# Transposing layer-normed rows by DMA instead of TensorE, and keeping split weights in DRAM, in a four-layer attention kernel

## The chip, the cores and the metric

The kernel runs on one core of a Trainium2 chip. The metric is the device time of one execution in microseconds (us), as the median of several runs. Profiles come from one further execution, recorded by the hardware profiler.

The core has five engines with instruction queues of their own: PE (TensorE, the matrix engine; its weight loads are a row of their own, PEld), DVE (VectorE), ACT (ScalarE), POOL (GpSimd) and SP (which here only issues DMAs). An engine takes its instructions strictly in order. Semaphores make it wait for the others.

## The reference

Four layers of multi-query attention over x of 2048 rows by 512 columns, 32 heads of 16 dimensions, one key head and one value head shared by all. Layers 0 and 2 use the weights A, layers 1 and 3 the weights B.

```python
def layer(x, wq, wk, wv, wo):                    # x: 1, 2048, 512
    q = (x @ wq).reshape(B, S, 32, 16).transpose(0, 2, 1, 3)
    k, v = x @ wk, x @ wv                        # one head of 16 each
    p = softmax(einsum("bhqd,bkd->bhqk", q, k) * 16 ** -0.5)
    o = einsum("bhqk,bkd->bhqd", p, v)
    return o.transpose(0, 2, 1, 3).reshape(B, S, 512) @ wo

x = x + layer(layernorm(x), A); x = x + layer(layernorm(x), B)
x = x + layer(layernorm(x), A); x = x + layer(layernorm(x), B)
```

All is float32. The softmax needs 4 x 32 x 2048 x 2048 exponentials.

## The kernel before

**Number formats.** A float32 operand of a projection is split into two float16 parts, high and low (`hi = float16(w)`, `lo = float16(w - hi)`). A product of two such operands is three float16 matmuls per chunk of 128 (`three`, L538). Probabilities and values stay float32.

**Units of attention.** The rows are four blocks of 512 queries, the heads four groups of eight, which makes 16 "pairs" per layer and 64 in all. Scores are computed in *halves*: a tile of 128 by 1024 float32, 64 halves to a pair, 4096 in all. A half goes one of two ways. With `score` (L858) PE writes one of two buffers `st` of PSUM and ACT takes the exponential into one of 16 tiles `pt` (L868). With `score_v` (L875) PE writes the bank `by_v` in two parts, and DVE works out the exponential: L902 twice, then a chain of five instructions (L916, L918, L919, L920, L913). `pv` (L928) multiplies the tiles `pt` with the values into two accumulators `acc`. Its matmuls, like those of the scores, use one 64-row half of the PE array each, and `both` (L519) issues work for the two halves together, so that they run beside each other.

**Everything else** goes through one more PSUM bank, `beside`: the projections for keys and values (kv), for the queries (one product per block and head group), the output projections, and, before the change, the transposes of x. A product is 12 float16 steps on each half of the array, taken step by step between the scores, or 12 whole-array steps (`whole`, L562). DVE must empty the bank before the next item may use it.

**Layer norm** of one block (`add_normed`, L592): for each of four tiles of 128 rows, DVE takes the statistics, POOL the power for the standard deviation, and DVE writes the normed rows `xn` (`norm`, L415). PE transposes each tile by four 128 by 128 float32 transposes into `beside` (`transposes`, L423). DVE then reads the bank twice: it writes the high part of `xnT` (L432) and subtracts to get the low part (L434). The first block of layer 0 has a path of its own ahead of the rest; 15 blocks, or 60 tiles, go through `add_normed`.

**Weights.** `add_load` (L580) loads a matrix (`wq` for the queries, `wo` for the output) in four chunks of float32, and DVE splits each chunk (`w_hi` L372, `w_lo` L377); the columns of `wq` are also reordered, and its low part takes four instructions. Since layers 2 and 3 use the same matrices as layers 0 and 1, and SBUF holds one set, each is loaded and split again there. `wq` of layer 0 is made ahead of the main part.

**The order** of the work is written out by hand in one string, `ORDER` (L58): each letter is a step, and the Python code that builds the kernel walks along it once. "S" is a score by ACT. Lower-case letters are pairs of actions for the two array halves: "E" and "O" stand for pv, "M" and "N" for one or two product steps, "V" and "W" for score_v (so "a" is pv on both halves, "l" and "m" on one, "p" and "q" a product step on one, "r" and "s" score_v on one). "P" is a whole-array product step, "F" another whole item on PE (a transposed tile, the transposes for v, query lengths), "X" the next item of DVE's list, "I" DVE's L902, "0" and "1" the next step of a DVE chain, "Q" the load of the next pair's queries, "G" and "D" the emptying of accumulators and the division, "Y" a read of `beside` by DVE that lets a bank change array halves. `plan` (L710) makes the two lists, for PE and DVE, from which P, M, N and F, and X, take the next item; an item names how far the other list must be. The string fixes each engine's own order; between engines only the data dependences count.

**DMAs.** Nearly all are issued by SP, in the order of the string. `spaced` (L807) spreads a row of them: the later ones are issued some exponentials later, each made to wait for an exponential shortly before. Queries go through DRAM (`q_rest` L479 stores them, `load_q` L821 loads them replicated). x lies in DRAM between uses (`load_x` L394, `out_add` L499).

Of the kernel before, what the change touches and what calls it, by code (L numbers as in the profile page):

```python
# [63 lines left out]
    "pSbm0SppspmSIppmpSYGeoSGrqqqlSIql0qqSc0lqS0maSa0lSpmppmXSlmSQXaXaSXFXSmaXXlXXSX0eqSlqqlqSrqqqlSYmIdpGpSp"
    "sdpSpmppSpImdpSYlGqqlS0qqaXSaXlSm0ap0SdnSQd0ppmSpmp0ppSmapSYlmqSlqqqlSrqolSqqlqSIqeXaSaXSadpSGppmSYGieIq"
    "Sem0Se0qlqS0qlmSQc0lqSma0SlmlqSlYmpSmpppmSkbISpmlXSfXaSIalSGpmpd0SpmnGSpppS0pm0bSa0lSmaSQ0lqqeSqlqqSclqS"
    "qaSclmSXaXSfaSlmlIsSImlSGFSXXa0aS0lmqSXqlXmlSGqlqqS0aaSQXa0SpmppmXpSb0pSpmdXpSXpdYlSqgqqSXXlmXeSqlmSqalX"
    "GSmqSXaaXSaIqSlGqqqrScIeSYm0ap0SQb0pSpmpmp0SbnmS0dlSmalSsYqlqSqIclXSmaSXalSpmppmSpGYmlSqqGrcISc0lqSoe0Sl"
    "0maSQl0mSppmpmDDp0SpmppSdaSYqelSmfXlXSaIpSdppsSpmIdpSpmYl0Sqqc0lSGmqSGc0lqSqqlqSDlmDaDSQlmS0almSDDb0pSda"
    "SYqalSXmgXSaIaSlmrSFSIXlmfGSppmInSGppspS0pmIaS0dl0SsalSQ1mdp0SalS1ma1Sqee0SqcS0aeSqqlIqS0lmmrSeIlqSGmmrS"  # L70
    "0aIaSGglS0daISXaS1mgXlSm1ap1SpmnSm0ndSppmDpS0bmlSmDlDSlm0lmSloIqSc0eSqqrlDDqS0qlmScIlmXSmrXlSmlIpm0Snm0s"
    "pSpmIppSpm0aSls1dS0alSb1mS1alSm0aScIeSDqqeS0qalSDqqlDjSmIaS0alSmk0lS0maS0lmlSIqqlmXSlmXlSm0ppmSpbDD0Spmr"
    "pmSIppmpSY0lsmlIqSql0mS0clqSml0jSqqlqISQa0aSa0Smr0aS0qalSqlDmS0qlmlSmDlDmSaIlSGdpmSXagGSlSXlmIa0SFSXrmlS"
    "XpmppmSppmpSpm0dpSIpmpp0Slm0lmSlmXX0SccXSql0qqSceXSqlsqSDDlmIaXSlm0Smg0lS0maSaIlS0marSIlmS0lmmlS0mgS0alS"
    "Ima0SrmlISlm0lmSrml1Sma0Sa0lSmIaS0gmlSIaS0mglS1ma0SlmS0alm0SmSIa0aSrmSIa0lmSrmlS0maISaXgSmS0mIal0SslmS1l"
    "mSQ0aa1SS0aaISSGrlGSIma0lSslm0SalSm1aS0lmSIalm0SrmXSIlmml0SrS1a0aSS1a0aSlmISlm0SmalXSsSXmaIlSXmlsSaXSaaS"
    "SXXaa0SqqqS1qel0qSqoS0cIeSm0aSrmlISpmn0mrSdn1Sd0bSb0pSmlXa0SpmnSbId0SppsdSIppm0pSmlgS0mlISql0qqlq0SqrqeS"
    "IloqS0qilSXmaS1ppm0ppSmpppmISpm0ppS0malS0mrlSqqloISqe1eSQ0oreSql0mS0almSlImS0pmpgSmIaS0gmlSImeSGllSXXrmG"
    "mSIaXlSsDlmSX0lmmlDDSmlS1maXlS1mlSX0aXaS0lmSaXXlmSlm1SlmmXl0SmlS1almSX0lmSaIaSDDlmXSXF0SfaISaXlSXsaSXF0S"
    "XalmISlmXrSXXFISXmlsS0aXaS0FSlSXXaS0PPPS1PP0SPPP0SP0PSPPSImaXlSXmlSXmlXFXSlmXrSXXmXlXImpS0ppmrSma1lS0mlS"  # L80
    "qlq0loISeq0qSqal0SqqeSa0aSQlmDSpmlDmpDSsppmIpSpmp0pSkmlISma0l0SmrlSqIlmSXagXSml1mpS1ppmpSGlpSGb1dSal0Spm"
    "dS1alSm0aSqlIqlqS0qcrSqqlIqSl0mfS0al0qSqlmSIlml0qSslmSIal0mSpspmSXlmlXSml0pmS0pmnS0pmppmS0pmlSpmdIlS0mlr"
    "SmlImSDDc0jS0ce0SqqlqSIeml0SqlmS0qglmSlmISYmg0nSXmaSXlml0Spm0bSppmIpSpm0aSpmlDSpmDlmDrSmpIlSm0lsSa0lmS0q"
# [1366 lines left out]
```

## Time and profile before

| | before |
|---|---|
| median of 3 runs | 3433.49 us (3431.62 to 3435.33) |
| the profiled execution's own time | 3427.37 us |
| its span, first to last instruction | 3425.6 us |
| granted TensorE clock | 1.000 |
| busy: PE, DVE, ACT | 3357.2, 3251.7, 3382.0 us |
| exponentials on ACT, halves on DVE | 3658, 438 |
| DMA | 147.81 MB, mean 43 GB/s |
| first exponential starts | 24.70 us |

A row of a group of instructions reads: line, engine, operation, output <- input, shape, count | busy time in us, mean length of one in ns | idle time of the engine just before them, and what ended it. Lengths of instructions overlap on an engine (an exponential lasts 1102 ns, the next one starts earlier), so a busy time is not count times length. In a table by stage, each engine has its busy time and, in brackets, the number of its instructions. A row of waits reads: who waited <- for whom, us in total, times, longest. A row of the timeline: start, length, engine, line, what, count, and in square brackets the idle time before it.

### The profile page before, as it was taken

The page shows a single profiled execution, that of the slowest core. Times are in us where ns is not written, and L with a number is a line of the kernel's source. Part 1 is how long each engine was busy: PE and PEld are TensorE (multiplying, and loading weights), DVE is VectorE, ACT ScalarE, POOL GpSimd, SP SyncE. Part 2 cuts the span into 40 slices and gives each one's busy share as a digit, 9 for nine tenths or more (in the row PEclk, how much of TensorE's full clock was granted, in tenths as well). Part 3 has the DMA queues.
Part 4 walks back from the last instruction along what each step waited for, and adds up shares of the span by engine and source line. Part 5 has one row for each costly group of instructions (what it writes and reads, how often), then busy time and mean ns, then how long its engine had stood idle before and what let it go on. Part 6 is the DMA issues. An engine that isn't in the chain of part 4 may idle for free.

```text
span 3425.6 us, 206570 instructions
## 1 busy us (share of the span) xinstructions
PE 3357.2 (98%) x97707; PEld 2087.9 (61%) x97707; DVE 3251.7 (95%) x4436; ACT 3382.0 (99%) x3688; POOL 133.3 (4%) x137
## 2 busy tenths in 40 slices
PE   9999999999999999999999999999999999999998
PEld 5666566555566766646556666664646666554554
DVE  7889999999999999999998999999999899999998
ACT  8999999999999999999999999999999999999997
POOL 3000000000000000000000000000000000000000
PEclk9999999999999999999999999999999999999999
DMA  3221011011012111101001211110101211111010
GB/s 111 63 80 48 32 42 46 28 33 41 30 46 61 49 49 39 42 23 45 23 30 58 59 48 38 42 43 23 47 19 36 67 47 37 35 48 31 23 43 21
DMA packets 119315, 147.81 MB, mean 43 GB/s; under 512 B 32888, under 2 KB 81016, under 8 KB 118456
## 3 DMA queue, kind: packets, MB, share of 16 engines
q1 hardware_dynamic: 116888, 133.65, 13.3%
q8 instruction: 765, 12.53, 1.5%
q10 hardware_dynamic: 1568, 0.85, 0.1%
q14 instruction: 94, 0.77, 0.1%
HBM read 90.57 MB, written 34.59 MB: 37 GB/s over the span
## 4 chain that ended last, share of the span: by engine, by line
PE 60%; ACT 26%; DVE 10%; issue 2%; DMA 1%; SPq 0%; DVEq 0%; ACTq 0%
PE acc L532 31%; ACT pt L868 26%; PE st L532 16%; PE beside L532 9%; PE by_v L532 2%; DVE pt L902 1%; DVE poly L919 1%; DVE poly L920 1%; DVE pt L913 1%; DVE mant L916 1%; PE beside L426 1%; DVE pt L918 1%; PE beside L569 0%; DMA rec<-rs 0%; SPq L1051 0%
## 5 line engine op out<-in xcount | busy, mean ns | idle before, releaser
L868 ACT ACTIVATE pt<-st 128x1024 f32<-128x1024 f32 x3658 | 3367.8, 1102 | 18.4 <-PE st L532 14.4
L532 PE MATMUL acc<-pt,vop 64*32 64x256 f32 (+1 forms) x51728 | 2888.1, 434 | 3.0 <-DVE sum L1017 2.0
L532 PE MATMUL st<-qt,kop 64*32 64x512 f16 x29264 | 1756.6, 380 | 46.1 <-ACT pt L868 25.2
L532 PEld LDWEIGHTS acc<-pt,vop 64*32 64x32 f32 x51728 | 1328.0, 106 | 248.6 <-DVE sum L1017 11.5
L532 PEld LDWEIGHTS <-kop 64*32 64x32 f16 x32768 | 794.3, 90 | 921.5 <-issue 643.7
L902 DVE TENSOR_SCALAR pt<-by_v 128x512 int32<-128x512 f32 x876 | 597.0, 681 | 33.1 <-PE by_v L532 28.2
L913 DVE SCALAR_TENSOR_TENSOR pt<-poly,pt 128x1024 f32<-128x1024 f32 x438 | 535.4, 1222 | 3.4
L920 DVE SCALAR_TENSOR_TENSOR poly<-poly,mant 128x1024 f32<-128x1024 f32 x438 | 534.7, 1222 | 3.1
L919 DVE SCALAR_TENSOR_TENSOR poly<-mant 128x1024 f32<-128x1024 f32 x438 | 533.5, 1219 | 0.0
L532 PE MATMUL beside<-xnT,wq 64*32 64x512 f16 x5760 | 437.4, 376 | 1.6 <-DVE qs L481 0.4
L532 PE MATMUL beside<-wo,ot 64*32 64x512 f16 x5472 | 406.1, 376 | 0.6 <-DVE gqk L497 0.3
L532 PE MATMUL by_v<-qt,kop 64*32 64x512 f16 x3504 | 350.6, 376 | 3.3 <-DVE pt L902 1.8
L918 DVE TENSOR_SCALAR pt<-pt 128x1024 int32<-128x1024 int32 x438 | 303.9, 694 | 4.6
L916 DVE TENSOR_SCALAR mant<-pt 128x1024 int32<-128x1024 int32 x438 | 301.0, 688 | 6.3
L532 PEld LDWEIGHTS <-wq 64*32 64x32 f16 x5760 | 169.8, 92 | 49.1 <-issue 11.7
L532 PEld LDWEIGHTS <-ot 64*32 64x32 f16 x5472 | 159.5, 92 | 40.0 <-issue 5.0
L477 POOL TENSOR_TENSOR sq<-qs 128x512 bf16<-128x512 f16 x64 | 73.6, 1150 | 872.1 <-DVE qs L474 872.1
L532 PE MATMUL beside<-xnT,wkv 64*32 64x512 f16 x1344 | 97.7, 376 | 0.0
L1017 DVE COPY sum<-acc 128x512 f32<-128x512 f32 x126 | 84.0, 686 | 12.0 <-PE acc L532 8.7
L413 POOL TENSOR_TENSOR rstd<-var,nhalf 128x4 f32<-128x4 f32 x15 | 21.7, 1445 | 1451.5 <-DVE var L412 1451.5
L474 DVE TENSOR_SCALAR qs<-beside 128x512 f16<-128x512 f32 x62 | 42.6, 688 | 18.1 <-PE beside L532 9.1
L998 DVE COPY seen<-beside 128x1 f32<-128x1 f32 x92 | 14.3, 155 | 40.4 <-PE beside L532 35.2
(124 smaller groups left out, 831.0 us busy)
## 6 DMA issues: line engine op xcount, KB each, us to landing
qt<-qs SPq DMA_DIRECT2D x236, 128.0 KB
qs<-qs SPq DMA_DIRECT2D x127, 128.0 KB
rec<-rs SPq DMA_DIRECT2D x63, 256.0 KB
qt<-qs SPq DMA_DIRECT2D x26, 512.0 KB
xs<-xt SPq DMA_DIRECT2D x48, 256.0 KB
xt<-xs SPq DMA_DIRECT2D x48, 256.0 KB
sum<-sum SPq DMA_DIRECT2D x252, 32.0 KB
xt<-in_A_x_dram SPq DMA_DIRECT2D x30, 256.0 KB
```

The source lines that it names most:

```text
L426: PE.transpose(ps[:, c * P:(c + 1) * P], xn[:, c * P:(c + 1) * P], ident)
L474: V.tensor_scalar(qs[:, 0], ps, BIG, -BIG, ALU.min, ALU.max)
L477: G.tensor_tensor(sq, qs[:, 0], qs[:, 0], ALU.mult)
L532: PE.matmul(o[32 * j:32 * j + 32], w[j][h], x[j][h], start=start, stop=stop, skip_group_check=True, tile_position=(64 * r, 32 * j))
L868: e = A.activation(pts[:, i], st[s], AF.Exp, scale=SCALE / UP / UP).ins
L902: w = V.tensor_scalar(e[:, 512 * r:512 * r + 512], by_v, SCALE / UP / UP * LOG2E * 2.0 ** 23, LEAD, ALU.mult, ALU.add).ins
L913: writer[i] = V.scalar_tensor_tensor(p, poly, C0, p, ALU.add, ALU.mult).ins
L916: lambda: V.tensor_scalar(mant.bitcast(I32), e, 0x3FFFFF, 0x3F800000, ALU.bitwise_and, ALU.bitwise_or),
L918: lambda: V.tensor_scalar(e, e, 0x7FC00000, HALVES, ALU.bitwise_and, ALU.bitwise_or),
L919: lambda: V.scalar_tensor_tensor(poly, mant, C2, mant, ALU.add, ALU.mult),
L920: lambda: V.scalar_tensor_tensor(poly, poly, C1, mant, ALU.add, ALU.mult),
L1017: V.tensor_copy(sums[pr, odd], acc[odd])
```

## The change

It has four parts.

**Transposes.** The normed rows `xn` are split in SBUF: DVE casts them to float16 (`row_hi`), and later subtracts (`row_lo`). Each of the two parts, 128 rows by 512 columns, is transposed by a DMA of SP into its place in `xnT` (`turned`). PE's transposes and their use of `beside` go. `norm` and the list of `add_normed` are regrouped in pairs of tiles.

**Weights.** Split parts are stored in DRAM the first time (`keep_w`, one store per chunk and part; for `wq` of layer 0 all eight, spaced by three exponentials, at the start of the main part). For layers 2 and 3 `reload_w` loads the eight pieces, spaced by two exponentials, and DVE does nothing.

**Room.** A pool `rws` is added, and the room reserved for dynamic DMAs (`dynamic_dma_scratch_size`) is set to 4096. No DMA of the kernel is issued by POOL.

**The order.** `ORDER` is new throughout. Counted by letter, old to new: S 3658 to 3657, X 772 to 740, F 93 to 33, P 72 to 108, Y 92 to 101, I 876 to 878, G, D and Q unchanged. The two strings begin and end as follows.

```
old: QXPPPPPPPSSPPPPPSXmXlSPPSPPSPPSPPsSPPSIPPSXflmXSaIlSm0aS0FXSmaXlSXmlXSQmaXXlS
new: QXSSPPPPPPSPPPSmrISPPPSmXlsSXlmIeSqqlqSq0e0lq0SqqclS0mSlm0mlSpmbSpmppSYmllqSQ
...
old: SmlIlSDsaISlm0mrSlSD0mal0Sa0SlmSIlm0mSlsS0lmaISa0Slm0Sa0aSS0maS0lmalDaa
new: Sa0SrmlmSIlm0gSa1Sa0lmSlm0Sa0aSa0SS0mSlmIlSmarSalSmaSlImalS000a0a0aa
```

```diff
+    rws = ctx.enter_context(tc.tile_pool(name="rws", bufs=4))
...
+    wscr = {(n, i): [scr.tile([P, NC, D], F16, name=f"{n}{i}{k}") for k in range(2)]
+            for n in ("wq", "wo") for i in range(2)}
+
+    def keep_w(key, c):
+
+        def save(c, k):
+            return lambda: SP.dma_start(wscr[key[0], key[1] % 2][k][:, c], wt[key][k][:, c])
+
+        spaced([save(x, k) for x in c for k in range(2)], 3 if len(c) > 1 else 0)
+
+    def reload_w(key):
+        begin_w(key)
+        spaced([lambda c=c, k=k: SP.dma_start(wt[key][k][:, c], wscr[key[0], key[1] % 2][k][:, c])
+                for c in range(NC) for k in range(2)], 2)
...
+    def turned(l, b, t, k, rows):
+        SP.dma_start_transpose(xnT[l, b][k][:, :, t * P:(t + 1) * P], rows)
+
+    def row_hi(l, b, t):
+        hi = rows_of[l, b, t] = rws.tile([P, D], F16, name="xhi")
+        V.tensor_copy(hi, xn_of[l, b, t])
+        turned(l, b, t, 0, hi)
+
+    def row_lo(l, b, t):
+        lo = rws.tile([P, D], F16, name="xlo")
+        V.tensor_tensor(lo, xn_of.pop((l, b, t)), rows_of.pop((l, b, t)), ALU.subtract)
+        turned(l, b, t, 1, lo)
...
     def add_load(key, chunks=range(NC)):
+        if key[1] >= 2:
+            return work.add_dve("wd", lambda: reload_w(key), 0)
         for c in chunks:
             if c == 0:
                 work.add_dve("wl", lambda: (load_w(key, 0), load_w(key, 1)), 0)
             work.add_dve("wh", lambda c=c: w_hi(key, c), 0)
-            work.add_dve("w", lambda c=c: (w_lo(key, c), c + 2 < NC and load_w(key, c + 2)), 0)
+            work.add_dve("w", lambda c=c: (w_lo(key, c), keep_w(key, [c]), c + 2 < NC and load_w(key, c + 2)), 0)
...
-        n0 = work.add_dve("xr", lambda: norm(l, b, 0), 0)
-        n1 = work.add_dve("xn", lambda: norm(l, b, 1), 0)
-        for t in range(4):
-            add_whole("t", lambda t=t: transposes(l, b, t, beside), n0 if t == 0 else n1)
-            work.add_dve("hi", lambda t=t: xnT_part(l, b, t, 0, beside))
-            n = work.add_dve("lo", lambda t=t: xnT_part(l, b, t, 1, beside), key=("end",))
-            n0 = n1
-            if t < 2:
-                n1 = work.add_dve("xn", lambda t=t: norm(l, b, t + 2), 0)
-            if t == 1:
+        for t0 in (0, 2):
+            for t in (t0, t0 + 1):
+                work.add_dve("xm" if t else "xq", lambda t=t: norm(l, b, t), 0)
+            if t0:
                 add_next_x(l, b)
+            for t in (t0, t0 + 1):
+                work.add_dve("xh", lambda t=t: row_hi(l, b, t), 0)
+            for t in (t0, t0 + 1):
+                n = work.add_dve("xo", lambda t=t: row_lo(l, b, t), 0)
         return n
...
     with tc.manual_schedule():
+        keep_w(("wq", 0), range(NC))
...
-    nc = _bacc.Bacc("TRN2", target_bir_lowering=False, num_devices=1)
+    nc = _bacc.Bacc("TRN2", target_bir_lowering=False, num_devices=1,
+                      dynamic_dma_scratch_size=4096)
```

More of the change, by code (lines that the diff above doesn't have):

```diff
@@ L64 @@
[L64 to L83, printed above, removed]
@@ new lines @@
+    "XaXSXFSXaXXXaXXSsSGlXGSXaIaSXlXmrSXmlImSXlmlXS0maX0Sa0lSmSXaXaXSQXSXaXaXSa0SaSGlGSXXml0SsalSXmXmXSaXlSIm"
+    "SrmIaSlS0a0a0SSa0aSQpmn0SmpppSpmdYlSqqeSqclSGqrGoSIceSsYpmnSmplmSIXaXSXmaXlSXFSXaXXXaX0Spm0ppSd0bSQpmp0p"
+    "Sbmp0SaaSlYGqqSqlqlqqSjeqSceSmImSGXaXlSsaqSqIeqlSq00loS0qelqSm0aSal0SQmndSdnSddpSpmppYSclSXmslXSaIlqSGqq"
+    "jSIqeaSq0eGeSo0eS0aaS0aSb0pmpSdnSQpmdpSppXmaSaXSalqqSqelqSqrqlqSqqlmSYGpdnISpmdSYGclsYSpIpmpSpmppmS0XalS"
+    "0maXlS0FSQXXlmS0bbS0bpSpmdpSpmYlSoiXlXSqcXSXcIeSqqlqSYlmXlmXSpmSGrlGSXmaXlXSmaSalSQmaXXlXSmlSIbdSY0eql0q"
@@ new lines @@
+    "Soe0SrqqeISoqS0lmml0SmSpkbSpImdpS0lGpSGdmXSa0lSXmlm0SQce0SqlqqScDD0lqSqaSYpbmpSppmpSpsmlSpmdpSYcIlSYmdlX"
+    "SmlXSaGcSqjGqSmDeISlqDmlDSQqlq0qSa0a0SaSpm0apSpmn0SmppspSDDmaIlSYqYrmlSqIlmSY0a0lsSdIaGSlpSGb0fSalSImlXm"
+    "SQl1fSXaDaS1FDSDmalXSml0Solqlq1SqloS0aeSmlImS0lmSpmGppkSGnpSId0aSlm0pSs0alSId0dSalS0rmlmSIqlqe0SqflS0maI"
+    "Slm0lS0mlmpSlXsmSIlmlXSrm1qlq0SqeqSql1ml1SmlqSqe0lqSma0SlmlISpm0lmSpsppmISpmp0pSspmp0pSd0dlSml0SalmISe0m"
+    "SlmrSIqalSXmfXlSm0eSIqel0qSql0mSqlm0lSqqlmS0ceSsaDDSYqlImlSrY0m0bS0pbSmnIdS0pmlkSpmIdSXlml1SQrmXlmS0ceSD"
@@ new lines @@
+    "qqeS0qeDlmDSqcIlSm0aSlmDDl0SpspmpSIpmd0pSslpmSGnm0pSllGSIma0pS0lmrSpmlImS0lmrSma0lSqlmXSlmIlSXma0SFDSDml"
+    "DmlSXmlSXmlqqlSqqlqSqe0lqS0oeSlm0aSlmXXS0pmpnsSImpppmXSps0pmpS0dlS0mapSaIlS0marSDDlqImS0agSaISXlmaSr0mlS"
+    "Imlm0Sf0lSa1aS0lmSa1aS0aSaIaS0mgSlmIlS0maSsa1l0SmlSlm0aISlm0Salm0SrmlSmIaSQ0agS0mSIa0aSGrSGllISm0aSflXS1"
+    "mal0SmlS1maS0alSImS0salISmS0rma1SlS0malISm0lsS0lmSaIa0SrSa1a0SSImalXSmlsSXlmSIa0aXSsSa0aSS0mal1Sml0SlmSI"
+    "a0aS0rSaIa0SrSaXaXSlmSlmXSlmmSlSXXa0bSpppSIpm0b0SppsmpISpml0SsalS1ml0Slqqql1qSql0oSce0ScSXlma0SqcSIqeDlq"
@@ new lines @@
+    "SQ0qqrqlSqcISlYm0h0Spmpp0SbdSIppmp0SpmdSXlmSGpmpGppsSppp0mSppmIpSpmdSY0cl0qSoj0lSqqlIqSc0eSmaXXSaDlDSmlX"
+    "mS0alsSmXlISXlmf0SlmX0lSmXaS0lmlSXmIlmS0alSXma0SlmlsXSXmIlS0lmmrS0lmlXSmIaS0alSmXaXSlXmXlSsXlmSIlmXml0Sf"
+    "lSm1aSXXa1lSXmmXS0alSImSXaXlsSImlmS0rmlSm1aS0lS1maS0lSIbb0SknSIdd0pSrmppSDDm1llS0mlS0eoe0SQqcSIce0SscSIl"
+    "mXaSXslmSGFXSXaXaSlSGXlmXXXaX0SppmpSDbpmDSnDmpSIbd0Sf0lSlImlm0SrqqlqS0qeqSqe0lqSqqlqS0lmXlmSXlmSDDb0dpIS"
+    "b0pSspbISpm0aSfl1Sml0lmSqlq0qSc0eSqcISc0lsSqlmISlDmf1SlmDlDSpmlm1SlXmSDDaXlm0SqlqqScIlq0SoeS0qelqSma0Sls"
@@ L230 @@
+    "aSaIaSGSGgl0SmImS0glmS1mS0malS1S0aaISa0SarSDDaIa0SsSa1a0SSIaa0Slm0SrmlSIa0aSsS1a0aSS0aIaDSlmDSDrmlSIa0aS"
+    "rS0aaS1lmS0lmSImal0SsS0malIS0sSa1aS0lmSlmISm0al0SrSImal1SsS0aa0SaSlm0SIa0aSrSIa0aSsS1a0aSSIa0aS0rmlSmlIS"
+    "1lmmS0rlSma0lSS0lmIaGSsSGllISm1aSr1mlS0almS1mSa0aSa0SlmSIlmmS0slSIlmml0SsaSIaSDD0rmaISlS00salSm1S0malS0m"
+    "lSaS0a0aSaISlm0rSlmImlS0rSmaIl0Smg0SlmISmg0lSmSD0SS0SD0aaDSaIa0Sa0SrmlmSIlm0gSa1Sa0lmSlm0Sa0aSa0SS0mSlmI"
+    "lSmarSalSmaSlImalS000a0a0aa"
 )
@@ L350, in fast_path @@
     stat = {}
-    xn_of = {}
+    xn_of, rows_of = {}, {}
     sq_of = {}
```

295 lines of the change are left out of this document (144 added, 151 removed).

## The prediction, made before the changed kernel was run

> **What bounds the kernel now.** I read the page's totals first, then the groups of instructions, then the busy time by stage, then the waits, and last the timeline of both ends.
>
> ```profile
> span 3425.6 us, 206570 instructions
> PE 3357.2 (98%) x97707; PEld 2087.9 (61%) x97707; DVE 3251.7 (95%) x4436; ACT 3382.0 (99%) x3688; POOL 133.3 (4%) x137
> ...
> PE 60%; ACT 26%; DVE 10%; issue 2%; DMA 1%; SPq 0%; DVEq 0%; ACTq 0%
> ...
> L868 ACT ACTIVATE pt<-st 128x1024 f32<-128x1024 f32 x3658 | 3367.8, 1102 | 18.4 <-PE st L532 14.4
> ```
>
> ACT is busy 99% of the span, nearly all of it in 3658 exponentials (L868). Yet the chain of waits goes through PE for 60% and through ACT for 26%: two full engines hand work to each other through two score buffers. How well this goes is seen by stage, in the column of ACT (busy, then count):
>
> ```profile
> core 0: us, PE busy (x) PEld busy (x) DVE busy (x) ACT busy (x) POOL busy (x), PEclk, DMA share, GB/s
> 25.00:1025.00 1000.00, 984.83 (x28888) 616.96 (x28894) 937.69 (x1309) 995.54 (x1082) 42.10 (x39) 1.00 0.16 48
> 1025.00:1225.00 200.00, 199.24 (x6295) 137.31 (x6293) 190.20 (x257) 198.43 (x215) 10.46 (x10) 1.00 0.20 55
> 1225.00:1925.00 700.00, 688.69 (x20002) 421.92 (x19984) 667.56 (x917) 696.91 (x758) 23.29 (x17) 1.00 0.14 40
> 1925.00:2325.00 400.00, 398.23 (x12471) 266.40 (x12458) 389.02 (x534) 398.23 (x433) 18.11 (x15) 1.00 0.16 44
> 2325.00:3025.00 700.00, 685.99 (x19761) 416.05 (x19751) 671.79 (x896) 697.85 (x760) 20.76 (x16) 1.00 0.14 39
> 3025.00:3405.00 380.00, 367.16 (x10113) 210.28 (x10101) 369.10 (x460) 379.54 (x415) 0.00 (x0) 1.00 0.10 31
> ```
>
> One exponential on each border is counted twice, so the paces are 1000/1081 = 0.925 us, 0.935, 0.925, 0.926, 0.922 and, in the last layer, 380/414 = 0.918. PE is busy 99.6% in the slowest stage and 96.6% in the quickest. If every stage ran at 0.918 instead of the mean 3380/3658 = 0.924, the kernel would win 3658 x 0.006 = 22 us. This is about all that relief of PE and DVE can give while ACT keeps its exponentials. Counted in the two order strings, these go from 3658 to 3657: DVE takes 439 halves instead of 438, though the change frees it.
>
> **The change part by part.** Profiled, the kernel took 3427.4 us (the span and 1.8 us around it); the median of the three timed runs is 6.1 us more. The sum is made on the first and carried over with that difference.
>
> *One exponential fewer on ACT*: -0.9 us, at the mean pace.
>
> *The start.* The old string issues seven whole-array products ahead of the first scores:
>
> ```profile
> 22.61 1.69 PE L569 MATMUL beside<-xnT,wq 128*128 128x512 f16 x7 [0.71 <-DVE gv L469]
> 24.22 0.63 PE L532 MATMUL st<-qt,kop 64*32 64x512 f16 x16
> 24.70 26.24 ACT L868 ACTIVATE pt<-st 128x1024 f32<-128x1024 f32 x28 [4.92 <-PE st L532]
> 24.78 1.25 PE L569 MATMUL beside<-xnT,wq 128*128 128x512 f16 x5
> 18.91 0.57 SPq L830 DMA_DIRECT2D qt<-qs  x1
> GB/s 0 0 0 0 0 0 183 156 342 19 0 0 0 0 55 284 371 393 284 11 44 205 208 186 58 0 0 0 0 197 229 415 339 300 339 322 246 240 164 186
> ```
>
> The new one begins with two scores. These need the query tile issued at 18.91; in the DMA rates (slices of 0.375 us from 15.0) its bytes end at 22.1 to 22.5. So the scores can start at 22.6 or 22.7, not 24.22: at most -1.6 us. Six products follow (seven took 1.69 us and five 1.25, so 0.22 each, 1.3 together), and the third score is ready when ACT has done two. I take -1.3.
>
> *Transposes leave PE.* Each of 60 row tiles loses four transposes:
>
> ```profile
> L426 PE MATMUL beside<-ident,xn 128*128 128x128 f32 x240 | 39.3, 286 | 0.9 <-DVE xn L420 0.3 <-DVE xnT L434 0.2
> PEld beside L426 <- DVE xnT L434: 7.9, 20, 0.6
> PEld beside L426 <- DVE xn L420: 7.6, 21, 0.6
> 1503.34 1.05 PE L532 MATMUL acc<-pt,vop 64*32 64x512 f32 x16
> 1504.41 0.63 PE L532 MATMUL acc<-pt,vop 64*32 64x256 f32 x16
> ```
>
> This is 39.3 us of PE work and up to 15.5 us of waits, which overlap other matmuls. How much reaches the end? I counted the two strings: 0.42 us for 256 columns of probabilities (1.05 - 0.63), 0.21 for a 512-column float16 step (0.22 each above), and in each interval between two scores the fuller of the array's two halves. The sum falls from 3347 to 3323 us, by 25. But intervals that hold over 1 us, more than ACT's period, rise from 2000 to 2039; what grew emptier are those that were empty already (0.21 us: 70 to 113). So relief comes where PE wasn't late. Bounds: -25 x 0.60, PE's share of the chain, is -15; 39 more crowded intervals at 1.07 - 0.92 = 0.15 give +6. I take -3, near the middle.
>
> *DVE work.* The high half is now read from SBUF, as in the row of L1059; the low half as in L1062, not from PSUM as now (L432, L434):
>
> ```profile
> L432 DVE CAST xnT<-beside 128x512 f16<-128x512 f32 x60 | 41.1, 685 | 3.3 <-PE beside L426 1.8
> L434 DVE TENSOR_TENSOR xnT<-beside,xnT 128x512 f16<-128x512 f32 x60 | 41.2, 686 | 1.3
> L1059 DVE CAST ot<-sum 128x512 f16<-128x512 f32 x63 | 26.5, 420 | 0.8
> L1062 DVE TENSOR_TENSOR ot<-sum,ot 128x512 f16<-128x512 f32 x63 | 44.2, 702 | 1.8
> L375 DVE TENSOR_SCALAR wq<-wst 128x512 f16<-128x512 f32 x12 | 9.2, 769 | 0.5 <-DMA wst<-in_B_wq_dram 0.5
> L375 DVE TENSOR_SCALAR wo<-wst 128x512 f16<-128x512 f32 x16 | 6.7, 420 | 3.0 <-DMA wst<-in_A_wo_dram 2.7 <-DMA wst<-in_B_wo_dram 0.3
> L381 DVE SCALAR_TENSOR_TENSOR wq<-wst,wq 128x128 f16<-128x128 f32 x48 | 16.0, 492 | 0.1
> L381 DVE SCALAR_TENSOR_TENSOR wo<-wst,wo 128x512 f16<-128x512 f32 x16 | 11.0, 689 | 0.4
> ```
>
> That is 60 x (0.685 - 0.420) = 15.9 us less and 60 x 0.016 = 1.0 more. Of the weights, two of three query sets and two of four output sets go: 2/3 x (9.2 + 16.0) + 1/2 x (6.7 + 11.0) = 25.7 us. Together -41; one more half of exponentials takes back 6.4 us (rows at the tail, below). DVE holds 10% of the chain: 0 to -4 us. I take -1, since most of the weight work stood in 1925 to 2325, a stage only 0.002 off the mean pace.
>
> *Weights in DRAM.* Eight stores of 128 KB for each of four sets, eight loads for each of four: no engine but SP issues them, and the DMA share is 0.10 to 0.20. The strings ask for the loads at scores 1242, 2015, 2161 and 2928 and use them 117 to 150 scores later, over 100 us. That cover hides all: 0; without it PE would stand for one load, some 3 us (the stores below), four times.
>
> *The transposing DMAs.* Two per row tile, 120 in all, issued by SP behind DVE's row_hi and row_lo. The first step of the kv product now waits for eight of them in place of DVE's last subtraction; behind that step on PE stand all scores, so ACT starves after two. On SP, query loads queue behind them, due some 15 exponentials later. No row shows a transposing DMA; the nearest are two plain stores of 128 KB:
>
> ```profile
> 15.93 0.71 SPq L483 DMA_DIRECT2D qs<-qs  x1
> 15.94 0.67 ACTq L483 DMA_DIRECT2D qs<-qs  x1
> ```
>
> In the rates above their bytes move from 17.25 to 18.75, and the query load that needs them is issued at 18.91: 2.8 to 3.0 us from issue. The new string leaves 6 to 9 scores (seven times 6) between the last row_lo and the kv product: 6 x 0.92 - 0.70 = 4.8 us at the tightest. I take 0; below nothing is excluded, since the kv step can't start before the string has it; above, late by d, it costs up to 15 x d. The Trainium skill is of two minds here. Its page "Advanced Engine Details and Errata", section X-Bar Transpose (TRN2), puts such DMAs on a par with plain ones, which leaves this term at 0; the rival on queued transposes has the other page.
>
> *The tail.* Old, seven scores follow the last score_v; new, four:
>
> ```profile
> 3399.35 6.63 ACT L868 ACTIVATE pt<-st 128x1024 f32<-128x1024 f32 x7
> L902 DVE TENSOR_SCALAR pt<-by_v 128x512 int32<-128x512 f32 x876 | 597.0, 681 | 33.1 <-PE by_v L532 28.2 <-PE st L532 2.0
> L918 DVE TENSOR_SCALAR pt<-pt 128x1024 int32<-128x1024 int32 x438 | 303.9, 694 | 4.6
> L913 DVE SCALAR_TENSOR_TENSOR pt<-poly,pt 128x1024 f32<-128x1024 f32 x438 | 535.4, 1222 | 3.4
> ```
>
> From score_v DVE needs 0.68 + 2 x 0.69 + 3 x 1.22 = 5.7 us (a whole half has a second 0.68: 6.4); four scores and the last exponential take 3 x 0.92 + 1.1 to 4 x 0.92 + 1.1, 3.9 to 4.8. So DVE ends last, by 1 to 2 us. I take +1.
>
> Sum: -0.9 - 1.3 - 3 - 1 + 0 + 1 = -5.2 us. Profiled 3422.2, median 3428.3: I say **3428**, 0.16% down. About 0.2% (6.9 us) is what a measurement of this kernel can tell from no change.
>
> **The rivals.**
>
> *PE is the bound.* For it: 60% of the chain, and the slowest pace where PE is busiest. Against it: 1225 to 1925 has PE at 98.4% and the pace of 25 to 1025. Then the whole -15 counts: -0.9 - 1.3 - 15 - 1 + 1 = -17, 3416.
>
> *The transposes land late (slower).* Place: the first kv step of 15 row blocks. It decides from 4.8 us after the last row_lo ends. At 7 us the seven blocks with 6 scores are late by 7.7 - 5.5 = 2.2 us, the seven with 7 by 1.3, the one with 9 not: 24 us, so 3428 + 24 = 3452. For it: transfers of 256 bytes per row and column block instead of 1 KB rows, and eight close together. Against it: plain stores have 2 us to spare.
>
> *They go one after another.* If each of a block's eight held the path for a store's 2.8 us, 22.4 us would pass from the first row_hi; the string has 13 to 33 scores up to the kv product, and summed over the blocks the lack is some 74 us: 3502. The Trainium skill, "VectorE: DVE Perf Modes", section The three transpose paths, speaks for this: it gives 1309 ns for a 128x128 transpose by DMA against 390 on TensorE and advises TensorE where PSUM will do. By it, as an estimate, a row half is four of these, 5.2 us, and the kernel would come near 3770.
>
> *The change doesn't do what it says.* If the cast from SBUF took 685 ns after all, DVE's relief were 25 us instead of 41, and the time 3429.
>
> **How the numbers follow.** Forecast 0.45 (own range 3420 to 3438: faster 0.11, same 0.31, slower 0.03); PE bound 0.30 (0.28, 0.02, 0); late 0.17 (0, 0.02, 0.15); one after another 0.04 (slower); the cast and the rest 0.04 (0.01, 0.02, 0.01). So faster 0.40, same 0.37, slower 0.23. The range 3408 to 3455 takes in the PE rival with its bounds and most of the late one.
>
> **What would show it.** The exponentials' pace by stage: 0.92 everywhere if I am right, below it in 1025 to 1225 and 1925 to 2325 if PE was the bound. First exponential at 23.2 us. No wait of PE for a DMA into xnT over 1 us in total per block; such waits, 15 times and over 2 us, would be the late rival, and queued ones over 5 us the next. DVE's cast at 0.42 us. I am wrong if stages without any kv product change their pace by over 0.005: then the new string itself, not its parts, made the difference.

## The result: 1.1% slower, and the profile after

| | before | after |
|---|---|---|
| median of 5 runs each, taken beside each other | 3431.62 us (3424.0 to 3435.33) | 3468.62 us (3466.5 to 3469.76) |
| ratio, 95% interval | | 1.0112 (1.0101 to 1.0123) |
| the profiled execution's own time | 3427.37 us | 3466.50 us |
| granted TensorE clock, mean | 1.000 | 0.995 |
| first exponential starts | 24.70 us | 25.45 us |

The change makes the kernel 37 us slower. The forecast was 3428, the range ended at 3455. First the page of the changed kernel: its span, its totals and the group of the exponentials.

```profile
span 3464.7 us, 203343 instructions
...
PE 3357.0 (97%) x95919; PEld 2045.8 (59%) x95919; DVE 3218.9 (93%) x4396; ACT 3385.9 (98%) x3687; POOL 137.6 (4%) x137
...
L895 ACT ACTIVATE pt<-st 128x1024 f32<-128x1024 f32 x3657 | 3371.5, 1100 | 50.2 <-PE st L559 43.5
```

The work is what was promised: 1788 matmuls and 33 us of DVE less, 3657 exponentials. But ACT now stands idle for 50.2 us between exponentials instead of 18.4, and 43.5 of that waits for PE's scores. PE is as busy as before with less to do, so something stretches its work. By stage (same columns as before):

```profile
core 0: us, PE busy (x) PEld busy (x) DVE busy (x) ACT busy (x) POOL busy (x), PEclk, DMA share, GB/s
25.00:1025.00 1000.00, 965.23 (x27589) 582.28 (x27590) 907.83 (x1285) 978.03 (x1060) 46.09 (x41) 1.00 0.23 58
1025.00:1225.00 200.00, 198.38 (x6151) 131.16 (x6143) 179.87 (x244) 196.74 (x213) 13.11 (x11) 1.00 0.22 60
1225.00:1925.00 700.00, 683.90 (x19586) 413.40 (x19567) 657.87 (x901) 693.23 (x755) 20.56 (x16) 1.00 0.18 45
1925.00:2325.00 400.00, 397.99 (x12255) 264.78 (x12254) 393.75 (x524) 399.82 (x436) 19.45 (x15) 1.00 0.20 50
2325.00:3025.00 700.00, 676.13 (x19334) 410.64 (x19319) 645.38 (x870) 685.46 (x744) 21.92 (x17) 0.99 0.16 42
3025.00:3405.00 380.00, 365.70 (x9876) 203.35 (x9868) 370.38 (x463) 379.54 (x414) 0.00 (x0) 1.00 0.11 33
```

Two stages lose most: the first does 1060 exponentials where it did 1082, the fifth 744 where it did 760. There PE is busy for less time than before, so it isn't the bound; it stands. The fourth gains three exponentials, and the last layer, which has no transposes, runs at 380/413 = 0.920 us instead of 0.918. The waits say what PE stands for:

```profile
ACT pt L895 <- PE st L559: 43.5, 36, 5.2
...
PEld L559 <- DMA xnT<-xlo: 12.9, 5, 5.6
...
PE beside L559 <- DMA xnT<-xlo: 12.2, 6, 5.1
...
PE by_v L559 <- DMA qt<-qs: 8.1, 3, 4.2
```

PE waits six times for a transposed low part, up to 5.1 us, and three times for a load of queries. I placed the loss by comparing, exponential by exponential, the start times in both traces: between the first and the last exponential the changed kernel loses 38 us. Three late blocks make up 21 of them (6.0 us around exponential 1954, 7.7 around 2629, 7.5 around 2866), layer 0 from exponential 30 to 100 makes 9.6, exponentials 180 to 200 make 4.7, the first ten 2.4; the rest nearly cancels, with gains of 3.4 between 2010 and 2250 and of 2.6 between 800 and 1060.

The worst place, the third block of rows for layer 3, in the timeline of the changed kernel:

```profile
2470.93 0.68 DVE L460 TENSOR_TENSOR xlo<-xn,xhi 128x512 f16<-128x512 f32 x1
...
2473.75 1.22 SPq L451 DMA_TRANSPOSE xnT<-xlo  x1
...
2475.05 1.18 SPq L1075 DMA_DIRECT2D rs<-den  x2
...
2476.29 2.79 SPq L1078 DMA_DIRECT2D sum<-sum  x4
...
2479.20 0.67 SPq L1082 DMA_DIRECT2D rec<-rs  x1
...
2480.31 0.34 SPq L412 DMA_DIRECT2D xt<-xs  x1
2480.70 1.24 SPq L451 DMA_TRANSPOSE xnT<-xlo  x1
...
2484.94 0.61 PE L559 MATMUL beside<-xnT,wkv 64*32 64x512 f16 x4 [5.06 <-DMA xnT<-xlo]
...
2486.07 1.02 ACT L895 ACTIVATE pt<-st 128x1024 f32<-128x1024 f32 x1 [5.18 <-PE st L559]
...
2487.77 1.02 ACT L895 ACTIVATE pt<-st 128x1024 f32<-128x1024 f32 x1 [0.68 <-PE st L559]
...
2489.48 1.03 ACT L895 ACTIVATE pt<-st 128x1024 f32<-128x1024 f32 x1 [0.68 <-PE st L559]
```

DVE ends the last `row_lo` at 2471.61. SP issues its transpose at 2480.70, 9.1 us later: until then it issues, in program order, earlier transposes, the seven DMAs of a division, and a load of x. PE can start the kv step at 2484.94, 4.2 us after the issue. Then come exponentials 1.7 us apart. The granted clock (the column PEclk, third from the right) explains these; the rows are of a table by window:

```profile
1855.00:1859.00 4.00, 4.00 (x68) 1.87 (x60) 0.16 (x1) 1.02 (x1) 0.00 (x0) 0.57 0.27 98
2484.00:2490.00 6.00, 5.06 (x88) 2.56 (x96) 1.27 (x2) 2.57 (x3) 0.00 (x0) 0.50 0.25 85
```

In this stand and behind it, PE has half clock for the whole six us; behind the stand at the late block before it (exponential 1954), for most of four. Here a late DMA is paid twice: as the wait, and as slow matmuls behind it.

How long a DMA holds SP is in the view by tile. First the transposing ones of the changed kernel, then the plain query loads before (shortest, median, longest in ns):

```profile
L451 SPq DMA_TRANSPOSE xnT<-xhi x60: 1188/1220/2967, 54.5 to 2703.3; - x60
L451 SPq DMA_TRANSPOSE xnT<-xlo x60: 1189/1220/2594, 57.3 to 2706.9; - x60
```

```profile
L830 SPq DMA_DIRECT2D qt<-qs x26: 513/550/568, 18.9 to 2716.6; - x26
```

Each transposing DMA takes SP 1.22 us, a plain one 0.55. The eight of a block are 9.8 us of SP, where plain ones would be 4.4.

### The profile page after: what moved, and what is told of

Same layout as the page of the kernel before. It is cut to its first block, busy times and chain, and to the rows that moved or that the text cites. A ratio compares the mean times of both kernels' runs of the same rounds, so it can differ in the third digit from the quotient of the medians.

```text
span 3464.7 us, 203343 instructions
## 1 busy us (share of the span) xinstructions
PE 3357.0 (97%) x95919; PEld 2045.8 (59%) x95919; DVE 3218.9 (93%) x4396; ACT 3385.9 (98%) x3687; POOL 137.6 (4%) x137
## 5 line engine op out<-in xcount | busy, mean ns | idle before, releaser
L895 ACT ACTIVATE pt<-st 128x1024 f32<-128x1024 f32 x3657 | 3371.5, 1100 | 50.2 <-PE st L559 43.5
L559 PE MATMUL st<-qt,kop 64*32 64x512 f16 x29256 | 1775.3, 380 | 63.9 <-ACT pt L895 40.0
L559 PEld LDWEIGHTS acc<-pt,vop 64*32 64x32 f32 x50432 | 1297.2, 106 | 241.2 <-DVE sum L1044 8.9
L559 PEld LDWEIGHTS <-kop 64*32 64x32 f16 x32768 | 803.1, 90 | 990.8 <-issue 721.1
L947 DVE SCALAR_TENSOR_TENSOR poly<-poly,mant 128x1024 f32<-128x1024 f32 x439 | 537.5, 1225 | 3.6
L559 PEld LDWEIGHTS <-wq 64*32 64x32 f16 x5856 | 170.7, 92 | 59.8 <-issue 18.4
L559 PE MATMUL beside<-xnT,wkv 64*32 64x512 f16 x1056 | 82.0, 407 | 13.5 <-DMA xnT<-xlo 12.2
L427 POOL TENSOR_TENSOR rstd<-var,nhalf 128x4 f32<-128x4 f32 x15 | 20.8, 1387 | 1387.0 <-DVE var L426 1387.0
```

Of the source, the lines that this page charges most:

```text
L427: G.tensor_tensor(r, var, nhalf, ALU.pow)
L559: PE.matmul(o[32 * j:32 * j + 32], w[j][h], x[j][h], start=start, stop=stop, skip_group_check=True, tile_position=(64 * r, 32 * j))
L895: e = A.activation(pts[:, i], st[s], AF.Exp, scale=SCALE / UP / UP).ins
L947: lambda: V.scalar_tensor_tensor(poly, poly, C1, mant, ALU.add, ALU.mult),
```

## The experiments

My theory after the result was that SP is held too long by each transposing DMA. The rivals were that the transposes land late whatever SP does, that the new order itself costs the time, and that the weights in DRAM do. All ratios stand against runs of the kernel before beside them, with 95% intervals. Of each edit only the lines that matter are shown, and of the order strings their beginnings.

**The transposing DMAs left out.** DVE writes both parts straight into `xnT`, untransposed, so the rows stand in wrong places; all else is the changed kernel.

```diff
-        V.tensor_copy(hi, xn_of[l, b, t])
-        turned(l, b, t, 0, hi)
+        V.tensor_copy(xnT[l, b][0][:, :, t * P:(t + 1) * P], by_chunk(xn_of[l, b, t]))
```

> The changed kernel with the transposing DMAs left out: DVE writes both parts of the normed rows straight into xnT, untransposed, so the kernel computes with wrongly placed rows; the new order, the DVE work and the weights in DRAM stay. Theory SP (each transposing DMA holds SP for 1.2 us where a plain one takes 0.55, so transposes and the query loads behind them come late, PE stands, and its granted clock is halved for some us after each stand): all of the loss comes back, 3424 to 3434 us, no clock under 1.00 after the first 100 us. Rival ORDER (the new order is the slower one by itself): 3455 us or more. Rival WEIGHTS (the stores and loads of the split weights cost it): 3460 us or more.

Measured 3441.04, ratio 1.0035 (1.0021 to 1.0048). Seven tenths of the loss go with the DMAs, but not all: the theory missed a part. (It also expected full clock behind the first 100 us; half clock comes once more, at 212.) What is left stands in the trace at the start (3.9 us in the first ten exponentials) and at exponentials 180 to 200 (4.6). Both can be seen in the changed kernel's timeline:

```profile
27.02 0.55 SPq L857 DMA_DIRECT2D qt<-qs  x1
...
30.97 0.40 PE L559 MATMUL by_v<-qt,kop 64*32 64x512 f16 x4 [2.10 <-DMA qt<-qs]
```

```profile
218.87 0.43 DVE L374 TENSOR_SCALAR wo<-wst 128x512 f16<-128x512 f32 x1 [2.56 <-DMA wst<-in_A_wo_dram]
...
220.68 0.65 PE L559 MATMUL acc<-pt,vop 64*32 64x256 f32 x4 [2.33 <-DVE sum L1046]
```

The new string's first score_v comes so early that it needs the second pair's queries, issued 4 us before. And `keep_w` puts its stores on SP ahead of the next chunk's load: DVE waits for the chunk, and PE for the sum that stands behind it on DVE.

**The weights alone**, in the old order without the 32 letters X of the later splitting.

```diff
+        if key[1] >= 2:
+            return work.add_dve("wd", lambda: reload_w(key), 0)
```

> The kernel before, with its old order, its transposes on PE, and only the weights in DRAM; the 32 DVE steps that this saves are struck from the old order. Theories SP and ORDER: the time of before, less 0 to 5 us for 26 us less DVE work, 3426 to 3433 us. Rival WEIGHTS: 3445 us or more.

Measured 3432.36, 1.0005 (0.9996 to 1.0014). The weights are no cause.

**The loads of x put behind the last row_lo**, in the changed kernel.

```diff
-            if t0:
-                add_next_x(l, b)
             for t in (t0, t0 + 1):
                 n = work.add_dve("xo", lambda t=t: row_lo(l, b, t), 0)
+        add_next_x(l, b)
```

> The changed kernel with one move: the loads of the next block's x, of which three wait for an exponential each, are queued on SP behind the block's eight transposes instead of between them. Theory SP: the transposes of the blocks where such a load stood in between are issued up to 5 us sooner, the stands of PE around scores 1954, 2629 and 2866 shrink by half or go, and the time falls by 8 to 20 us, to 3449 to 3461. Rivals ORDER and WEIGHTS: no change beyond 4 us.

Measured 3451.67, 1.0070 (1.0055 to 1.0086): 0.4% comes back from the mere order of SP's queue, with not one transpose changed.

**One transposing DMA per row tile**, high and low part together (128 by 1024): 60 instead of 120, the same bytes.

```diff
+        V.tensor_tensor(rows[:, 1], xn_of.pop((l, b, t)), rows[:, 0], ALU.subtract)
+        SP.dma_start_transpose(both_parts[l, b][:, :, t * P:(t + 1) * P],
+                               rows.rearrange("p k n -> p (k n)"))
```

> The changed kernel with one transposing DMA per row tile for both parts, 128 rows by 1024 columns, 60 instead of 120. Theory SP, if SP's time is a price per DMA (1.2 us each): half of SP's work on transposes goes, and the time falls by 10 to 25 us. If SP's time goes with the size (2.4 us each): SP has as much to do, the high parts start later, and the time stays within 5 us or rises by up to 10. Rivals ORDER and WEIGHTS: no change beyond 4 us.

Measured 3446.03, 1.0051 (1.0035 to 1.0066). In its view by tile a DMA of twice the size holds SP hardly longer:

```profile
L458 SPq DMA_TRANSPOSE xnT<-xhl x60: 1232/1296/3297, 55.9 to 2683.7; - x60
```

**The weights alone, stores later**: behind all of a matrix's loads, three exponentials apart.

```diff
-            work.add_dve("w", lambda c=c: (w_lo(key, c), keep_w(key, [c]), c + 2 < NC and load_w(key, c + 2)), 0)
+            work.add_dve("w", lambda c=c: (w_lo(key, c), c + 2 < NC and load_w(key, c + 2), c + 1 == NC and keep_w(key, range(NC))), 0)
```

> The kernel before with the weights in DRAM, as in the second run, but the stores of a set are queued behind the loads of all its chunks and spaced by three exponentials, instead of one pair of stores ahead of each load. Theory SP: the 1.8 us between scores 180 and 200 and the 1.5 us between 1060 and 1120 that the second run lost to before go, the 2.5 us that it won between 2010 and 2250 stay: 3426 to 3431 us, 1 to 4 us under before. Rival (the stores' traffic itself costs it): as the second run, within 1 us.

Measured 3427.48, 0.9995 (0.9986 to 1.0004): at the expected time, yet not measurably faster. The 1.8 us that the stores cost at exponentials 180 to 200 in the run of the weights alone fall to 0.4.

**The mended version**: one DMA per tile, loads of x behind, stores later, the first score_v four scores later, and one division moved behind the transposes of the worst block.

```diff
-QXSSPPPPPPSPPPSmrISPPPSmXlsSXlmIeSqqlqSq0e0lq0S
+QXSSPPPPPPSPPPSmSPPPSmXlSXlmrIeSqqlsqISq0e0lq0S
```

> The changed kernel with one transposing DMA per row tile, the loads of x behind the transposes, the stores of the weights behind the loads and spaced, the first score_v four scores later (at the old place in time), and two steps of a division behind the transposes of one block. Theory SP: of the 15 us that the fourth run's profile lost to before, some 3 at the start, 5 between scores 180 and 200, 2 to 3 between 1060 and 1120 and 2 at the late blocks go: 3430 to 3437 us, no more than 5 us from before. Rival ORDER: 3440 us or more.

Measured 3443.55, 1.0042 (1.0028 to 1.0056): missed. The late blocks are mended, but the moved stores meet other transfers: PE stops for 1.9 us in the middle of a group of matmuls at exponential 10, where the profile gives no releaser and a DMA share of 0.72 over 25 to 36 us, and a query load at 217 queues behind a division and stores. What stops PE at exponential 10 is open.

**Plain DMAs in place of the transposing ones**, same places in SP's queue, same bytes; the rows again stand untransposed.

```diff
-        SP.dma_start_transpose(xnT[l, b][k][:, :, t * P:(t + 1) * P], rows)
+        SP.dma_start(xnT[l, b][k][:, :, t * P:(t + 1) * P], rows.rearrange("p (c n) -> p c n", c=NC))
```

> The changed kernel with each transposing DMA replaced by a plain one of the same 128 KB into the same places; the rows then lie untransposed, so the kernel computes with wrongly placed rows. Theory SP: a plain DMA holds SP for 0.55 us, not 1.22, so eight hold it for 4.4 us and not 9.8, and of the loss of 38 us half or more goes: 3441 to 3452 us. Rival LANDING (PE waits for the time that the data takes to arrive, not for SP): plain ones land hardly sooner, and the time stays over 3460 us.

Measured 3440.69, 1.0032 (1.0021 to 1.0043): as without any DMA, just under the range that was expected. A plain DMA into the same tile holds SP half as long:

```profile
L451 SPq DMA_DIRECT2D xnT<-xhi x60: 593/625/1624, 55.4 to 2673.5; - x60
L451 SPq DMA_DIRECT2D xnT<-xlo x60: 593/600/2027, 56.8 to 2676.9; - x60
```

**Each transposing DMA cut in two**: 240 of 128 by 256, the same bytes.

```diff
+        for c in (0, 2):
+            SP.dma_start_transpose(xnT[l, b][k][:, c:c + 2, t * P:(t + 1) * P],
+                                   rows[:, c * P:(c + 2) * P])
```

> The changed kernel with each transposing DMA cut into two of 256 columns, 240 instead of 120 over the same bytes. Theory SP, with a price per DMA: eight become sixteen of 1.2 us, 19 us of SP per block where the order leaves some 13: late in most of the 15 blocks, by 5 us and more, 3520 to 3620 us. If SP's time goes with the size (0.6 us for a half): as the changed kernel, within 10 us.

Measured 3588.64, 1.0461 (1.0442 to 1.0480).

```profile
L452 SPq DMA_TRANSPOSE xnT<-xhi x120: 1168/1238/2612, 54.1 to 2827.4; - x120
L452 SPq DMA_TRANSPOSE xnT<-xlo x120: 1167/1230/2805, 59.9 to 2833.2; - x120
```

A quarter of the columns of the one DMA per tile, and 1.24 us of SP against 1.30. In the 15 blocks the last transpose is now issued 4.6 to 20.4 us after the last `row_lo` has ended, where the changed kernel had 0.0 to 9.1. 60, 120 and 240 DMAs that move the same bytes give 1.0051, 1.0112 and 1.0461: the price goes by count.

**No transposing DMAs, start and stores mended.** The first run again (rows untransposed), with the mended start, the moved division, and stores 136 (first `wq`) or 44 exponentials later.

```diff
+            later.append((len(exps) + (136 if key == ("wq", 0) else 44) + 3 * i, dma))
```

> The new order with no transposing DMA (DVE writes the normed rows straight into xnT, untransposed, so the kernel computes with wrongly placed rows), the first score_v four scores later, and the stores of split weights moved behind the loads and out of the crowded stretches (136 exponentials after the start for the first set, 44 after the splitting for the others). Theory SP: what the first run still lost to before (some 4 us in the first ten scores, 4.6 between scores 180 and 200) goes, the 3 us won between 2010 and 2250 and the 2 won between 620 and 1060 stay: 3424 to 3432 us, the forecast's 3428 in it. Rival ORDER: 3438 us or more.

Measured 3433.36, 1.0016 (1.0007 to 1.0025): just missed. Without a single transpose, on PE or by DMA, the new order is still not below the kernel before.

**The mended version with the same later stores.**

> The sixth run's kernel (one transposing DMA per row tile, x loads behind) with the stores of the split weights moved out of the first 130 exponentials and out of scores 190 to 230, so that they no longer stand on SP or on the DMA engines beside the loads of x and of the queries. Theory SP: the 2.3 us that the sixth run lost in its first ten scores and the 3.2 us that it lost between scores 200 and 300 go: 3433 to 3439 us. Rival ORDER: as the sixth run, 3441 us or more.

Measured 3437.00, 1.0025 (1.0015 to 1.0035), as expected. This is the best version of the whole change, and still slower than before.

**The relief in the old order.** The weights with stores later, and only the 60 letters F of the PE transposes struck from the old string; DVE writes the parts untransposed.

```diff
-            add_whole("t", lambda t=t: transposes(l, b, t, beside), n0 if t == 0 else n1)
-            work.add_dve("hi", lambda t=t: xnT_part(l, b, t, 0, beside))
-            n = work.add_dve("lo", lambda t=t: xnT_part(l, b, t, 1, beside), key=("end",))
+            work.add_dve("hi", lambda t=t: row_hi(l, b, t), 0)
+            n = work.add_dve("lo", lambda t=t: row_lo(l, b, t), 0)
```

> The old order with only the 60 letters of the PE transposes struck out, weights kept in DRAM with the stores put later, and DVE writing both parts of the normed rows straight into their place untransposed (so the rows stand in the wrong places; no transposing DMA, no PE transpose). PE loses 39 us of work and DVE about 41 us, as in the change, but every other step stands where it stood. The theory that the relief is worth little, because PE and DVE were not late where they are relieved, expects within 7 us of the kernel before, with the forecast's term of -3 to -4 the likeliest: 3421 to 3431. The rival that the relief is worth its share of the chain (-15) and that the new order eats it expects 3411 to 3420, and the kernel without transposes in the new order, which stood 0.16% over before, would then owe some 20 us to the order. A time over 3432 would say that the relief itself does harm.

Measured 3427.84, 0.9993 (0.9984 to 1.0002): no measurable gain. Its page shows the relief, and how little ACT has of it; the page of the run with the weights alone and stores later stands behind it:

```profile
PE 3335.1 (97%) x97467; PEld 2066.3 (60%) x97467; DVE 3219.1 (94%) x4380; ACT 3381.0 (99%) x3688; POOL 133.4 (4%) x137
...
L890 ACT ACTIVATE pt<-st 128x1024 f32<-128x1024 f32 x3658 | 3366.7, 1105 | 20.3 <-PE st L554 16.2
```

```profile
PE 3359.0 (98%) x97707; PEld 2090.4 (61%) x97707; DVE 3232.1 (94%) x4380; ACT 3381.3 (99%) x3688; POOL 133.4 (4%) x137
...
L885 ACT ACTIVATE pt<-st 128x1024 f32<-128x1024 f32 x3658 | 3367.1, 1103 | 18.9 <-PE st L547 15.5
```

24 us less of PE, 13 less of DVE, and ACT waits as long as before.

**The real DMAs in the old order**, one per tile, with the change's room for dynamic DMAs and two buffers `xhl` for the rows (the run with one DMA per tile in the new order has four); otherwise the run above.

```diff
+        SP.dma_start_transpose(both_parts[l, b][:, :, t * P:(t + 1) * P],
+                               rows.rearrange("p k n -> p (k n)"))
```

> The old order again with the 60 letters of the PE transposes struck out and the weights kept in DRAM, now with the real transposing DMAs, in their cheapest form of one per row tile. The old string leaves only 1 or 2 scores between the last low part of a block and its first kv step, 0.9 to 1.9 us, where the new one leaves 6 to 9. The last DMA holds SP for 1.3 us and lands about 3 us after its issue, so each of 15 kv products would wait some 1.5 to 4 us, and ACT has one or two scores in hand: 15 blocks by 1 to 3 us, with the half clock behind the longer stands of PE, so 20 to 60 us over the kernel before: 3450 to 3490. This is the theory that the new order was the price of the DMAs. If the order had nothing to do with them, the time would stay within 15 us of the same order without DMAs: below 3443.

Measured 3516.27, 1.0256 (1.0238 to 1.0273): more than expected. Its waits:

```profile
ACT pt L893 <- PE st L557: 94.6, 62, 6.4
PE beside L557 <- DMA xnT<-xhl: 51.2, 12, 6.0
...
PEld L557 <- DMA xnT<-xhl: 21.5, 5, 5.7
```

Now every one of the 15 blocks is late: 15 intervals between exponentials are 3.7 to 7.5 us long, together 72 us over the usual 0.9. The order does matter to the DMAs: against the same order without any, these 60 cost 2.6% here (1.0256 and 0.9993) and 0.2% in the new order (1.0051 and 1.0035). Not all of the difference need be the order's: with two buffers, DVE waits eight times, 13.3 us in all, for a DMA to free one, and with four in the new order never. No run tells the two apart.

This trace also shows what the half clock costs, since not every stand brings it. Two stands of nearly the same length, and the rows by window behind them (PEclk third from the right):

```profile
650.86 0.40 PE L557 MATMUL beside<-xnT,wkv 64*32 64x512 f16 x4 [3.24 <-DMA xnT<-xhl]
...
1884.58 0.40 PE L557 MATMUL beside<-xnT,wkv 64*32 64x512 f16 x4 [3.32 <-DMA xnT<-xhl]
```

```profile
651.00:654.00 3.00, 3.00 (x112) 2.59 (x102) 3.00 (x4) 1.95 (x3) 0.00 (x0) 1.00 0.03 5
1885.00:1888.00 3.00, 3.00 (x60) 1.91 (x52) 3.00 (x4) 1.02 (x1) 0.00 (x0) 0.50 0.00 0
```

Against the run before it, the 40 exponentials around the first stand lose 3.3 us, those around the second 5.1. So it is with all 15: the three stands without half clock lose their own length and at most 0.4 us more, the other twelve 1.4 to 3.6 us more, 2.3 on the mean.

## Why the prediction was wrong

**The step that failed** is "The transposing DMAs ... I take 0". I priced such a DMA by the landing of a plain store, 2.8 to 3.0 us, and set that against 4.8 us of slack, counted from the last row_lo. Landing was not what failed: at the three worst blocks the kv step starts 2.9 to 4.2 us after the last transpose is issued, up to 1.2 us more than I had but still within the 4.8. What had no term is the time between row_lo and the issue. I even wrote that query loads queue behind the transposes, but not that the transposes themselves queue: behind each other (1.22 us each, against 0.55 for a plain DMA), and behind the division and the loads of x that the string puts between. In the block shown, 9.1 us go by before the issue; 4.8 of them are the division's seven DMAs, more than the transposes' share. The runs bear this out from three sides: the same queue with plain DMAs has no loss (1.0032 against 1.0035 with none), moving the loads of x takes back 0.4%, and the loss goes by the number of DMAs, not by their bytes.

That gives a rival the right place and the wrong cause. "The transposes land late" expected 15 late blocks by 1.3 to 2.2 us and 3452. Three blocks and layer 0 are late instead, by up to 5 us, and the half clock adds to each. The lateness is uneven because what stands between transposes on SP differs from block to block. In layer 0 the query load is the one that comes late, behind four transposes:

```profile
99.40 2.53 SPq L451 DMA_TRANSPOSE xnT<-xhi  x2
102.03 3.19 SPq L451 DMA_TRANSPOSE xnT<-xlo  x2
105.31 0.55 SPq L857 DMA_DIRECT2D qt<-qs  x1
```

PE then stands 4.2 us for these queries, at 111.17.

**One after another (3502).** The DMAs do follow each other, but at 1.2 us of SP and not at a store's 2.8. The sign set for this rival, a wait of over 5 us, came once (5.06). The Trainium skill's price in "VectorE: DVE Perf Modes", section The three transpose paths, is for one 128 by 128 block; taken per block, a DMA of 1024 columns would need eight times 1309 ns, 10.5 us as an estimate. The trace disagrees. With one such DMA per tile in the old order, the kv step starts 4.2 us after the issue:

```profile
2190.92 1.24 SPq L458 DMA_TRANSPOSE xnT<-xhl  x1
...
2195.11 0.61 PE L557 MATMUL beside<-xnT,wkv 64*32 64x512 f16 x4 [5.99 <-DMA xnT<-xhl]
```
The Trainium skill's other page, "Advanced Engine Details and Errata", section X-Bar Transpose (TRN2), which puts these DMAs on a par with plain ones, agrees roughly for the landing here (2.9 to 4.2 us, against 2.8 to 3.0 for the plain stores to DRAM; no row has the landing of a plain DMA into this tile), and not for SP: 1.22 us against 0.60 to 0.63 into the same tile.

**Transposes leave PE, -3, and DVE, -1.** The forecast of a small gain fits, and it is too small to measure: with all the relief in the old order, the ratio is 0.9993, -2.4 us, with an interval from -5.5 to +0.7. The rival "PE is the bound" (-15) falls with it. DVE's rows came nearly as forecast (cast 419 ns for 420, subtraction 686 for 702, 33 us less in all), so "the change doesn't do what it says" falls too. One local gain is real: exponentials 2010 to 2250, where the later weights were split, are 2.4 to 3.5 us quicker in every kernel that keeps them in DRAM; other places give it back.

**Weights, 0.** Right as a sum (1.0005). The stores ahead of the loads were not costed: exponentials 180 to 200 lose 4.7 us in the new order and 1.8 in the old, and with the stores later 1.4 to 1.7 and 0.4 to 1.2.

**The start, -1.3.** The first exponential came at 25.45, not 23.2. In three runs of the new order it did come at 23.15 to 23.28. What differs is the clock ahead of it, first in the changed kernel, then in the mended one without transposes:

```profile
9.00:15.00 6.00, 5.55 (x37) 4.69 (x37) 5.09 (x14) 4.34 (x12) 5.70 (x14) 0.50 0.18 31
```

```profile
9.00:15.00 6.00, 4.64 (x62) 3.92 (x61) 5.13 (x15) 4.69 (x12) 5.70 (x13) 1.00 0.19 31
```

The old order has both cases too: the first exponential starts at 24.70 and 24.89 with full clock in the prologue, and at 26.22 to 26.28 in three runs with half clock for 3.4 us. So with full clock on both sides the new start is 1.4 to 1.7 us earlier, about as forecast; that the profiled execution before had the full clock and the one after had not looks like chance, since both orders have both. Why the prologue has the half clock in some executions and not in others is open. Where the gain came, the early score_v gave it back (2.1 us of wait in the rows above).

**The tail, +1, and one exponential fewer** came as forecast: from the start of the last exponential to the end of the span it is 21.9 us instead of 20.8, and PE waits for DVE's last half (0.46 us, at 3445.40). In the twelve later traces, too, this stretch is 21.8 to 22.1 us in the new order and 20.5 to 20.9 in the old.

**The sign for the order itself**, a pace changed by over 0.005 in stages without a kv product, told nothing clear: the last layer changes by 0.002, and 1025 to 1225 goes to 200/212 = 0.943 from 0.935, with stores of `wo` in it (exponentials 1101 to 1112) and 0.004 to one exponential.

Put together, the ratios to the kernel before:

| order | transposing | ratio |
|---|---|---|
| old | none (relief alone) | 0.9993 |
| old | 60 DMAs | 1.0256 |
| new | none | 1.0035 |
| new | none; start and stores mended | 1.0016 |
| new | 120 plain DMAs | 1.0032 |
| new | 60; x loads, start, stores mended | 1.0025 |
| new | 60 | 1.0051 |
| new | 120; x loads behind | 1.0070 |
| new | 120 (the change) | 1.0112 |
| new | 240 | 1.0461 |

From 1.0035 to 1.0112 is the price of the DMAs, 26 us. From 0.9993 to 1.0035 is that of the new order, with the weights' stores where the change puts them, 14 us: 0.0019 of it go with the mended start, stores and division. The remaining 0.0023 is 8 us by the medians and 5 between the first and the last exponential of the two traces; cut into 29 equal stretches, these differ most in the second (exponentials 127 to 254, 2.9 us), and by 1.8 or less in each other. Which of the order's choices cost it is open. The share of the half clock in the 26 us is not isolated in this order; at the three late blocks of the changed kernel, PE stands for 10.9 of the 21 us, and the rest goes with 17 us of half clock.

## What to carry to other kernels

Price a DMA twice: by its landing, and by the time for which it holds the queue that issues it, times the number in the stretch, with everything that stands between them in program order. When an engine is relieved, first look whether it was late there: 98% busy did not make PE the bound, and taking 24 us from it gave nothing that could be measured. A move that needs slack takes it from the order, and here the new order, even without the DMAs, cost 14 us, more than the whole relief gave; how much of that is the slack itself is open.

## What the runs showed of the hardware

- A transposing DMA from SBUF to SBUF holds SP for 1.24, 1.22 and 1.30 us at 256, 512 and 1024 columns of 128 rows; a plain one into the same tile for 0.60 to 0.63.
- A stand of PE of 2.2 us was enough for the granted clock to fall to a half behind it, in a kernel that kept PE 97% busy. The Trainium skill, "TensorE: Matmul & The Clock Gate", section What's actually happening, lets it fall after an idle window of about 3.4 us; here a shorter stand did it:

```profile
1854.85 0.40 PE L559 MATMUL beside<-xnT,wkv 64*32 64x512 f16 x4 [2.21 <-DMA xnT<-xlo]
...
1856.66 1.02 ACT L895 ACTIVATE pt<-st 128x1024 f32<-128x1024 f32 x1 [3.49 <-PE st L559]
```

The clock of that place is the row 1855 to 1859 above, 0.57 on the mean of four us.

- The length of a stand alone doesn't decide. With one DMA per tile, a stand of 1.68 us (up to 1063.3) halved the clock; in the old order one of 3.24 us (up to 650.9) did not. In the clock records of all 14 traces, half clock outside the prologue begins on a fixed grid of 3.41 us and lasts one or more of its steps. Between 30 and 3380 us, wherever PE was idle for 1.97 us or more of a step at full clock, the next step had half clock (38 of 38); below 1.6 us it never had; between, in 3 of 11. The 3.24 us fell into two steps, 1.69 and 1.63.
